# Seven products for part of the second expert chunk, with its sums of x made earlier, and a later spread of the first w2 maxima

## The chip, the cores and the metric

One core of a Trainium2 chip runs the whole program. The metric is the device time of one execution in microseconds (us); the median of three executions of the kernel before is 957.64 us (957.54 to 958.07).

## What is computed

The input is 2 x 8 heads of 768 tokens and 64 features. Attention inside clusters gives 1536 tokens of 512 features; a mixture of four experts and a second two-layer network follow. Cut to what matters here:

```python
x = attention(q, k, v, centroids)                  # 1536 x 512
p = domain_probs / domain_probs.sum(-1)            # 1536 x 4
for e in range(4):                                 # first network
    h = np.maximum(x @ w1[e], 0.0)                 # 1536 x 1024
    out += p[:, e:e + 1] * (h @ w2[e])
h = out @ w_in                                     # second network, 1536 x 2048
return np.maximum(0.01 * h, h) @ w_out
```

## The kernel before, in words

**Numbers.** Products of the two networks are made of 16-bit halves. A 32-bit matrix is scaled by a power of two, rounded to its high half on ScalarE (ACT), and the low half is the difference, made on GpSimd (POOL) or VectorE (DVE). Each product is then three matmuls on TensorE (PE): high x high, high x low, low x high. The scale comes from the largest entry: `peak` (L220, ACT) takes the maxima of each partition, `peak_across` (L224, PE) spreads them over the partitions with one small matmul, `peak_top` (L228 and `power`, DVE) takes the maximum of these and its power of two, and `weights_split` (L272, then `split_halves`, L264 and L267) scales and splits the weights.

**Chunks.** The hidden features are worked in chunks of 256: `N1` = 16 chunks of the experts (chunks 0 to 15) and 8 of the second network. A chunk has a first layer (x by w1, ReLU times p in `h_act`, L790 or L822, then halves of h in `split`, L139 and L140) and a second layer (`emit_y1`, L1195 to L1197: 12 blocks of 128 features by 512 tokens, each of six matmuls of 512 columns, copied or added into `acc` at L1203 and L1205).

**Two forms of the first layer.** In the plain form (`plain`, L1070) a chunk is 72 matmuls of 512 columns. In the form with seven products (`emit_seven`, `product`, L1059) w1 and x are seen as 2 x 2 blocks, x by halves of the features and by halves of the tokens (768 each), and seven products of blocks take the place of eight. It needs four sums of blocks of w1 (`weights_sums`, L284 to L287 on POOL, then their halves on ACT and POOL) and four of x (`input_sums`, L1013 on DVE, their high halves L1016 on ACT). The sums of x stay the same for all expert chunks. Before the change chunks 0 and 1 are plain and chunks 2 to 15 have seven products for all tokens. Two chunks of the second network have a mixed form (`full` is false): seven products for the 512 first tokens of each half (set A, 42 matmuls of 512 columns), plain ones for the other 256 of each half (set B, `plain_b`, L1119, 24 matmuls).

**Order.** Nothing is scheduled by a planner in this part: each engine works through its instructions in the order in which the program issues them, and waits on semaphores. Attention is written as a time line: `at(when, step)` entries, sorted by `when`; the pairs of constants in `PEAK_AT` place the maxima pass and the spread of chunk 0's w1 and w2 there. Chunk 0's first layer for tokens 0 to 1023 runs inside this time line (`h_products`, L775; `h_finish_early`, L822); its third block, tokens 1024 to 1535, is plain and comes after the attention pool `main` was closed (`st_main.close()`). Then the pool `ffn` is opened over the same memory; `raw64`, `sums`, `thi`, `tlo`, `part` and `acc_n` lie there. The temporaries `f` and `g` of `input_sums` are the two `raw64` tiles.

Between the blocks of a first layer and of a second layer the loop at the end of the kernel drops `steps`: small closures that carry the preparation of the next chunk and of the sums. `quota` says how many of the sums go into which stretch. In the second layer of a chunk whose successor has no spread inside `emit_seven` (`L1_POINT` false, as for chunk 0), the spread of the next w1's maxima follows the second block:

```python
emit_y1(c, i)
if i == (3 if c == N1 else 1) and more and not L1_POINT(c):
    peak_across(0, bank(1 if c == N1 - 1 else 6 if c == N1 or c >= FULL else 0))
    peak_top(c + 1, 0)
    weights_split(c + 1, 0)
```

Before the change the sums of x are 18 steps of 2 x 768 columns: 9 in the second layer of chunk 0, 6 in the first layer of chunk 1 and 3 in its second layer.

Of the kernel before, what the change touches and what calls it, by code (L numbers as in the profile page):

```python
# [8 lines left out]
F32 = mybir.dt.float32  # L9
# [4 lines left out]
AF = mybir.ActivationFunctionType  # L14
# [36 lines left out]
NORM_LAST = (6.49, 6.57)  # L51
PHI_LAST = ((0, 2, 4), (0, 2))
SPLIT_AT = (3.6, 7.0, 12.5)
PEAK_AT = ((4.6, 8.2), (18.1, 21.0))
FILL = ((0, 0, 1.07), (0, 6, 1.08), (0, 12, 6.38), (0, 18, 6.39), (1, 0, 9.94), (1, 6, 10.27), (1, 12, 10.27))

BIG = float(2 ** 60)
# [18 lines left out]
def attention_moe_kernel(  # L76
# [13 lines left out]
    nc = tc.nc  # L90
    B, H, S, D = q.shape
    C = centroids.shape[1]
    NT, DM = out.shape
    E, _, FE = w1.shape
# [12 lines left out]
    HT = NT // 2  # L107
# [67 lines left out]
    hbuf, gbuf, pbuf = [], [], []  # L175
# [3 lines left out]
    N1 = len(chunks)  # L179
# [3 lines left out]
    def weights_load(c, part):  # L183
        wa, wb, f0, e = chunks[c]
        r, n = (raw64, 2) if wide and e is None else (raw12, 1)
        if part == 0:
            src = wa[:, n * f0:n * (f0 + FCH)]
        else:
            src = wb[f0:f0 + FCH, :]
        nc.sync.dma_start(out=r[part], in_=src.rearrange("(k p) f -> p k f", p=128))  # L190
# [418 lines left out]
    def scaled_split(hi, lo, src, by):  # L609
# [12 lines left out]
        out=ident, in_=ident, pattern=[[1, 128]], compare_op=ALU.is_equal, fill=0.0,  # L622
# [6 lines left out]
    def warm(n):  # L629
# [10 lines left out]
        out=both.rearrange("p (t c) -> p t c", c=2 * C), in0=iv[:, :, 0, :], in1=iv[:, :, 1, :], op=ALU.add,  # L640
# [4 lines left out]
        out=par, in_=ident.rearrange("p (a h c) -> p h a c", h=2, c=C), op=ALU.add, axis=AX.XY,  # L645
# [12 lines left out]
        out=cw[:, 3:4], in0=cw[:, 0:1], scalar=cw[:, 2:3], in1=cw[:, 1:2], op0=ALU.mult, op1=ALU.add,  # L658
# [4 lines left out]
    for h in range(2):  # L663
        nc.vector.tensor_scalar(
            out=cpad[:, h, :], in0=craw, scalar1=cw[:, 5:6], scalar2=par[:, h:h + 1], op0=ALU.mult, op1=ALU.mult,
        )
    ps = small()
# [14 lines left out]
    for n in range(1, NQK):  # L682
# [11 lines left out]
        out=dp.rearrange("p (b j) e -> p b (j e)", b=B),  # L694
        in_=probs.rearrange("(b p j) e -> p b (j e)", b=B, j=J),
# [13 lines left out]
    steps = prep_argmax(0, 0)  # L709
# [3 lines left out]
    steps = prep_argmax(0, 1)  # L713
# [74 lines left out]
    def h_act(c, g, src, p):  # L788
        if c < N1:
            nc.vector.scalar_tensor_tensor(out=g, in0=src, scalar=0.0, in1=p, op0=ALU.max, op1=ALU.mult)  # L790
        else:
            nc.scalar.activation(out=g, in_=src, func=AF.Prelu, scale=H_DOWN, alpha=0.01)
# [9 lines left out]
    def like(x, y):  # L802
        return x if len(y.shape) == 2 else x.rearrange("p (u t) -> p u t", u=2)
# [75 lines left out]
    for pr in range(NPAIR):  # L879
        o = 2 * J * pr  # L880
        at(o + 3 * J + (X_AT if pr != NPAIR - 2 else X_LAST), emit_X, pr)
        if pr > 0:
            m = V_MOST_AT[pr]
# [78 lines left out]
    acc_n = ffn.tile([128, NTILE, DM], F32, name="accn")  # L962
# [3 lines left out]
    def is_wide(c):  # L966
        return wide and chunks[c][3] is None

    raw64 = [
        ffn.tile([128, KC, 2 * FCH], I32, name="w1raw64"), ffn.tile([128, FCH // 128, 2 * DM], I32, name="w2raw64"),  # L970
    ]
# [4 lines left out]
    part = ffn.tile([128, 2, NT // 2], F32, name="part")  # L976
# [22 lines left out]
    quarters = [[x[:, 2 * k:2 * k + 2, HT * u:HT * u + HT] for x in (xhi, xlo)] for k in range(2) for u in range(2)]  # L999

    t_hi, t_lo = [[t[:, 0], t[:, 1], quarters[1][n], t[:, 2]] for n, t in enumerate((thi, tlo))]

    def input_sums():

        sub, add = ALU.subtract, ALU.add
        b11, b12, b21, b22 = quarters
        f, g = [
            x.bitcast(F32).rearrange("p a b -> p (a b)")[:, 0:NT].rearrange("p (k t) -> p k t", k=2) for x in raw64
        ]
        e = part  # L1010

        def tt(out, in0, in1, op):
            return lambda: nc.vector.tensor_tensor(out=out, in0=in0, in1=in1, op=op)  # L1013

        def hi(n, src):
            return lambda: nc.scalar.activation(out=t_hi[n], in_=src, func=AF.Copy)  # L1016

        def lo(n, src):
            return tt(t_lo[n], src, t_hi[n], sub)

        return [
            tt(f, b12[0], b11[0], sub), tt(f, f, b12[1], add), tt(f, f, b11[1], sub),
            hi(0, f), tt(g, b22[0], f, sub), tt(g, g, b22[1], add), lo(0, f), hi(1, g), tt(e, b22[0], b12[0], sub),
            tt(e, e, b22[1], add),
            lo(1, g), tt(e, e, b12[1], sub), tt(f, b21[0], g, sub), tt(f, f, b21[1], add), hi(3, f),
            hi(2, e), lo(3, f), lo(2, e),
        ]

    def turn_sums(m):
# [44 lines left out]
    def emit_seven(c, steps, late):  # L1074
# [12 lines left out]
        u2, u3 = [{A: part[:, n, A], B: part[:, n, B]} for n in range(2)]  # L1087
        gB = [g_slot(2), g_slot(3)]

        full = c < N1 or c >= FULL  # L1090
        calls = [5 if full else 6]

        def some():
# [19 lines left out]
        def plain_b(f):  # L1113

            ps = bank(f)
            xs = [x.rearrange("p k (u t) -> p k u t", u=2) for x in (xhi, xlo)]
            for k in range(KC):
                for i, j in ((0, 0), (0, 1), (1, 0)):
                    nc.tensor.matmul(  # L1119
                        ps.rearrange("p (u t) -> p u t", u=2), lhsT=w[i][:, k, 128 * f:128 * f + 128],  # L1120
                        rhs=xs[j][:, k, :, 512:HT], start=k + i + j == 0, stop=k == KC - 1 and i == 1,
                    )
            h_act(c, gB[f], ps, None)
            hi, lo = [x[:, f, :].rearrange("p (u t) -> p u t", u=2)[:, :, 512:HT] for x in hbuf[0]]
            split(hi, lo, gB[f].rearrange("p (u t) -> p u t", u=2), nc.gpsimd)

# [151 lines left out]
    def mixed(*lists):  # L1278
        return [x for row in zip_longest(*lists) for x in row if x]

    PLAIN = (0, 1, N1, N1 + 1)
    FULL = N1 + 4
    sums_left, quota = [], []
    for c in range(NCH):
# [14 lines left out]
        if c in PLAIN:  # L1299
            if c != N1:  # L1300
                if c > 0:
                    weights_split(c, 1)
                out_scale(c)
            if c == N1:
                sums_left = turn_sums(slice(0, 512))
                quota = [0, 6, 4, 3]
            if c == 0:
                sums_left = input_sums()
                quota = [0, 9, 6, 3]
            n = quota.pop(0)  # L1310
            slots = mixed(sums_left[:n], steps)
            slots[len(slots) // 2:len(slots) // 2] = late[:1]
            if c != N1:
                slots += late[1:]
            sums_left = sums_left[n:]
            if c == N1:
                turn_max(1)
                for k in range(KC):
                    turn_split(1, k)
                weights_split(c, 1)  # L1320
            blocks = [(u, f) for u in range(2 if c == 0 else 0, NU) for f in range(NF)]
            for n, (u, f) in enumerate(blocks):
                if c > 0 and c != N1:
                    ps = bank(BANKS[u][f])
                    plain(c, u, f, ps)
                elif f == 0:
                    both_ps = [bank((BANKS[u] if c else LAST_BANKS)[f]) for f in range(NF)]
                    for k in range(KC):
                        for g in range(NF):
                            plain(c, u, g, both_ps[g], [k])  # L1330
                if c == N1 and n == 0:
                    turn_across(1, bank(1))
                    turn_scale(1)
                    for k in range(KC):
                        turn_split(2, k)
                    out_scale(c)
                if c == 0 or c == N1:
                    ps = both_ps[f]
                h_whole(c, f, ps, 512 * u, hl=[tokens(x[:, f], c, u, True) for x in hbuf[0]])
                if c == N1 and n < 2:  # L1340
                    continue
                for _ in range(-(-len(slots) // (len(blocks) - n))):
                    slots.pop(0)()
            left = []
        else:
            emit_seven(c, steps, late)
            left = steps

        steps, later = left, []
        if c == N1 + 2:  # L1350
            sums_left = turn_sums(slice(512, HT))
            quota = [5, 8]
        if c in PLAIN or N1 + 2 <= c < FULL:
            n = quota.pop(0)
            later, sums_left = sums_left[:n], sums_left[n:]
        if more:
            if not is_wide(c + 1):
                later.insert(0, lambda: peak(c + 1, 1))
            else:
                if c + 1 != N1:  # L1360
                    later.insert(0, lambda: peak(c + 1, 1))
                if c == N1:
                    later = late[1:] + later
                if c + 2 < NCH:
                    later.append(lambda: weights_load(c + 2, 1))
            if L1_POINT(c):
                steps.append(lambda: weights_split(c + 1, 0))
            else:
                steps.insert(0, None)
            if c + 1 not in PLAIN:  # L1370
                steps += weights_sums()
            if c + 2 < NCH and not is_wide(c + 2):
                steps.append(lambda: weights_load(c + 2, 0))
        if c == N1 - 3 and wide:
            steps += [lambda: weights_load(N1, 0), lambda: weights_load(N1, 1)]
        if c < N1 - 1 and c % (FE // FCH) == FE // FCH - 1:
# [66 lines left out]
```

## Time and profile before

| | us |
|---|---|
| median of three executions | 957.64 |
| the profiled execution | 957.70 |
| its span, first to last instruction | 955.8 |
| PE busy | 938.0 (98%) |
| DVE busy | 749.0 (78%) |
| ACT busy | 536.8 (56%) |
| POOL busy | 564.1 (59%) |

Times within the trace count from the start of the span. A row of a time line gives start, duration, engine, line, operation, what is written and read, the number of merged instructions, and in brackets how long the engine had stood idle and what released it. Matmuls overlap, so a row of PE may be longer than its share: a matmul of 512 columns lasts 0.38 us, and the next one starts 0.216 us after it did.

### The profile page before, as it was taken

Reading aid. Unit: us, or ns where it says so; the run is one execution under the profiler, and the core shown is the slowest. Engines: PE = TensorE matmul, PEld = TensorE weight load, DVE = VectorE, ACT = ScalarE, POOL = GpSimd, SP = SyncE. Lnnn points to the kernel's source line nnn. Section 1 sums busy time; section 2 is a strip of 40 time slices with the busy share of each in tenths; the row PEclk is TensorE's granted clock in tenths of the full one; section 3 lists DMA queues with packets and bytes.
Section 4 is the critical chain, followed back from the end, with each engine's and each line's share of the span. In section 5 each row is a group of like instructions: output and inputs, shape, how many; then the busy total and the mean of one; then the engine's idle time right before and its main releaser. Section 6 shows DMA issues by size and latency. Waiting matters only on the chain.

```text
span 955.8 us, 16375 instructions
## 1 busy us (share of the span) xinstructions
PE 938.0 (98%) x6423; PEld 552.2 (58%) x6456; DVE 749.0 (78%) x1286; ACT 536.8 (56%) x775; POOL 564.1 (59%) x456
## 2 busy tenths in 40 slices
PE   8899999999999999999999999999999999999998
PEld 5788888877545555555555555555544444455554
DVE  7989998889697676666766667666889978998865
ACT  3678777778555344334344343443579755566552
POOL 4467777780367565455654465654636667777672
PEclk9999999999999999999999999999999999999999
DMA  8785556550110112110211102114111211221103
GB/s 181 182 186 120 129 131 156 122 135 3 45 45 25 42 47 54 45 45 23 61 40 45 45 23 75 37 33 132 45 45 59 94 54 60 88 89 45 45 1 132
DMA packets 62245, 70.81 MB, mean 74 GB/s; under 512 B 28148, under 2 KB 44920, under 8 KB 62168
## 3 DMA queue, kind: packets, MB, share of 16 engines
q1 hardware_dynamic: 62168, 69.77, 27.0%
q8 instruction: 50, 0.82, 0.4%
q14 instruction: 27, 0.22, 0.1%
HBM read 46.19 MB, written 3.17 MB: 52 GB/s over the span
## 4 chain that ended last, share of the span: by engine, by line
PE 84%; DVE 11%; ACT 2%; DMA 1%; issue 1%; SPq 0%; DVEq 0%; ACTq 0%
PE z L1059 27%; PE z L1195 9%; PE z L1196 8%; PE z L1197 8%; PE z L1257 4%; PE z L1259 4%; PE z L1258 4%; PE z L1070 4%; PE big L508 3%; DVE m L512 2%; PE big L543 2%; PE big L544 2%; PE small L569 1%; PE small L570 1%; PE small L571 1%
## 5 line engine op out<-in xcount | busy, mean ns | idle before, releaser
L140 POOL TENSOR_TENSOR hlo<-g,hhi 128x512 bf16<-128x512 f32 x140 | 186.4, 1354 | 89.9 <-ACT hhi L139 89.9
L1205 DVE SCALAR_TENSOR_TENSOR acc<-z,outer,acc 128x512 f32<-128x512 f32 x180 | 133.8, 748 | 64.7 <-PE z L1197 64.7
L557 POOL TENSOR_TENSOR plo<-p,phi 128x768 f16<-128x768 f32 x83 | 136.2, 1652 | 68.3 <-ACT phi L556 38.6
L139 ACT ACTIVATE hhi<-g 128x512 f16<-128x512 f32 x140 | 86.6, 628 | 111.8 <-DVE g L790 110.2
L1195 PE MATMUL z<-hhi,w2hi 128*128 128x512 f16 x384 | 145.5, 379 | 1.6
L1196 PE MATMUL z<-hhi,w2lo 128*128 128x512 f16 x384 | 145.5, 379 | 0.0
L267 POOL TENSOR_TENSOR w2lo<-w2raw,w2hi 128x512 f16<-128x512 f32 x46 | 63.5, 1400 | 131.5 <-ACT w2hi L264 131.5
L1197 PE MATMUL z<-hlo,w2hi 128*128 128x512 bf16 x353 | 133.8, 379 | 0.0
L512 DVE TENSOR_REDUCE m<-big 128x1 f32<-128x768 f32 x96 | 89.9, 950 | 14.0 <-PE big L508 13.7
L546 ACT ACTIVATE p<-big 128x768 f32<-128x768 f32 x96 | 76.6, 808 | 34.6 <-PE big L544 28.6
L1059 PEld LDWEIGHTS <-shi 128*128 128x128 f16 x608 | 59.5, 98 | 41.3 <-issue 0.2
L1099 DVE TENSOR_TENSOR part<-z,part 128x512 f32<-128x512 f32 x76 | 41.2, 563 | 50.9 <-PE z L1059 48.3
L267 POOL TENSOR_TENSOR w1lo<-w1raw,w1hi 128x512 f16<-128x512 f32 x46 | 57.4, 1270 | 28.5 <-ACT w1hi L264 18.8
L1059 PE MATMUL z<-xx,shi 128*128 128x512 f16 (+1 forms) x304 | 73.1, 329 | 0.1
L1257 PE MATMUL z<-w2hi,hhi 128*128 128x512 f16 (+1 forms) x194 | 73.1, 377 | 0.1
L1059 PE MATMUL z<-xx,w1hi 128*128 128x512 f16 (+1 forms) x304 | 73.1, 329 | 0.0
L1259 PE MATMUL z<-w2hi,hlo 128*128 128x512 f16 (+1 forms) x194 | 73.1, 377 | 0.0
L1258 PE MATMUL z<-w2lo,hhi 128*128 128x512 f16 (+1 forms) x194 | 73.1, 377 | 0.0
L543 PE MATMUL big<-qka 128*128 128x512 f32 x192 | 70.0, 367 | 2.8 <-DVE m L512 1.2
L1266 DVE SCALAR_TENSOR_TENSOR accn<-z,outer,accn 128x512 f32<-128x512 f32 (+1 forms) x85 | 60.2, 736 | 14.5 <-PE z L1259 14.4
L264 ACT ACTIVATE shi<-sums 128x1024 f16<-128x1024 f32 x20 | 21.1, 1057 | 88.4 <-POOL sums L287 88.4
L790 DVE SCALAR_TENSOR_TENSOR g<-z,pb 128x512 f32<-128x512 f32 x92 | 51.7, 568 | 19.2 <-PE z L1059 11.4
(250 smaller groups left out, 2342.7 us busy)
## 6 DMA issues: line engine op xcount, KB each, us to landing
qkb<-pair SPq DMA_DIRECT2D x32, 384.0 KB
w1raw<-in_moe_w_dram SPq DMA_DIRECT2D x16, 512.0 KB
w2raw<-in_moe_w_dram SPq DMA_DIRECT2D x16, 512.0 KB
w1raw<-in_moe_w_in_dram SPq DMA_DIRECT2D x8, 1024.0 KB
w2raw<-in_moe_w_out_dram SPq DMA_DIRECT2D x8, 1024.0 KB
qka<-pair SPq DMA_DIRECT2D x16, 384.0 KB
qraw<-in_q_dram SPq DMA_DIRECT2D x16, 192.0 KB
kraw<-in_k_dram SPq DMA_DIRECT2D x16, 192.0 KB
```

Source lines behind the costliest of these rows:

```text
L140: lo_engine.tensor_tensor(out=lo, in0=src, in1=as_read(hi), op=ALU.subtract)
L267: nc.gpsimd.tensor_tensor(out=lo[:, x], in0=src[:, x], in1=hi[:, x], op=ALU.subtract)
L512: nc.vector.tensor_reduce(out=m_t[t][:, j:j + 1], in_=ps[:, 0:S], op=ALU.max, axis=AX.X)
L557: (nc.vector if plo_on_vector else nc.gpsimd).tensor_tensor(out=plo, in0=p, in1=phi, op=ALU.subtract)
L1059: nc.tensor.matmul(ps, lhsT=w[i][:, k, :], rhs=x[j][:, k, sub], start=first and k + i + j == 0, stop=k == 1 and i == 1, skip_group_check=True,
L1195: nc.tensor.matmul(out, lhsT=whi[:, f, ks], rhs=h, start=f == 0, stop=False)
L1196: nc.tensor.matmul(out, lhsT=wlo[:, f, ks], rhs=h, start=False, stop=False)
L1197: nc.tensor.matmul(out, lhsT=whi[:, f, ks], rhs=l, start=False, stop=f == NF - 1)
L1205: nc.vector.scalar_tensor_tensor(out=a, in0=out, scalar=by, in1=a, op0=ALU.mult, op1=ALU.add)
L1257: nc.tensor.matmul(ps, lhsT=hi[:, f, ts], rhs=whi[:, f, m], start=f == 0, stop=False)
L1258: nc.tensor.matmul(ps, lhsT=hi[:, f, ts], rhs=wlo[:, f, m], start=False, stop=False)
L1259: nc.tensor.matmul(ps, lhsT=lo[:, f, ts], rhs=whi[:, f, m], start=False, stop=f == NF - 1)
```

## The change

Chunk 1 gets the mixed form: seven products for set A (1024 tokens), plain ones for set B (512 tokens). The sums of x are made in two passes, first for set A (steps of 2 x 512 columns), then for set B (2 x 256 columns). The first five steps of set A are issued ahead of chunk 0's third block, the other 13 in chunk 0's second layer; set B has 8 steps in the first layer of chunk 1 and 10 in its second layer. Chunk 0's second layer also gets the sums of chunk 1's w1 and their halves, and chunk 2's w1 load goes behind them. The temporary `e` moves from `part` to `acc_n`, since `part` now holds products in chunk 1. The spread of chunk 0's w2 maxima goes from 21.0 to 23.9 in the time line of attention, from between two groups of the last head's output products to behind them.

```diff
-PEAK_AT = ((4.6, 8.2), (18.1, 21.0))
+PEAK_AT = ((4.6, 8.2), (18.1, 23.9))
...
-    def input_sums():
+    def input_sums(m):
 
         sub, add = ALU.subtract, ALU.add
-        b11, b12, b21, b22 = quarters
-        f, g = [
-            x.bitcast(F32).rearrange("p a b -> p (a b)")[:, 0:NT].rearrange("p (k t) -> p k t", k=2) for x in raw64
+        b11, b12, b21, b22 = [[x[:, :, m] for x in b] for b in quarters]
+        f, g, e = [
+            x.rearrange("p a b -> p (a b)")[:, 0:NT].rearrange("p (k t) -> p k t", k=2)[:, :, m]
+            for x in [*[r.bitcast(F32) for r in raw64], acc_n]
         ]
-        e = part
...
         return [
             tt(f, b12[0], b11[0], sub), tt(f, f, b12[1], add), tt(f, f, b11[1], sub),
-            hi(0, f), tt(g, b22[0], f, sub), tt(g, g, b22[1], add), lo(0, f), hi(1, g), tt(e, b22[0], b12[0], sub),
-            tt(e, e, b22[1], add),
-            lo(1, g), tt(e, e, b12[1], sub), tt(f, b21[0], g, sub), tt(f, f, b21[1], add), hi(3, f),
-            hi(2, e), lo(3, f), lo(2, e),
+            tt(g, b22[0], f, sub), hi(0, f), tt(g, g, b22[1], add), tt(e, b22[0], b12[0], sub), hi(1, g),
+            tt(e, e, b22[1], add), lo(1, g), tt(e, e, b12[1], sub), lo(0, f), hi(2, e),
+            tt(f, b21[0], g, sub), tt(f, f, b21[1], add), lo(2, e), hi(3, f), lo(3, f),
         ]
...
-        full = c < N1 or c >= FULL
+        full = 1 < c < N1 or c >= FULL
...
-            h_act(c, gB[f], ps, None)
+            if c < N1:
+                p = pbuf[0][:, 0, :].rearrange("p (u t) -> p u t", u=2)[:, :, 512:HT]
+                h_act(c, like(gB[f], p), like(ps, p), p)
+            else:
+                h_act(c, gB[f], ps, None)
...
-    PLAIN = (0, 1, N1, N1 + 1)
+    PLAIN = (0, N1, N1 + 1)
...
             if c == 0:
-                sums_left = input_sums()
-                quota = [0, 9, 6, 3]
+                sums_left = input_sums(slice(0, 512))
+                for _ in range(5):
+                    sums_left.pop(0)()
+                quota = [0, 16]
...
         else:
+            if c == 1:
+                sums_left = input_sums(slice(512, HT))
+                steps = steps[1:] + sums_left[:2] + steps[:1] + sums_left[2:8]
+                quota = [10]
+                sums_left = sums_left[8:]
             emit_seven(c, steps, late)
...
-        if c in PLAIN or N1 + 2 <= c < FULL:
+        if c < 2 or c in PLAIN or N1 + 2 <= c < FULL:
             n = quota.pop(0)
...
+            if c == 0:
+                steps = [None] * 4 + steps[1:5] + steps[6:] + [None] * 4 + steps[5:6]
```

## Rows read from the trace of the kernel before

**Rows 1.** The page, part 1: busy time of each engine.
```profile
PE 938.0 (98%) x6423; PEld 552.2 (58%) x6456; DVE 749.0 (78%) x1286; ACT 536.8 (56%) x775; POOL 564.1 (59%) x456
```

**Rows 2.** Windows: busy time and count per engine, granted clock, DMA share, GB/s.
```profile
250.00:260.00 10.00, 9.95 (x47) 4.56 (x47) 4.70 (x10) 5.75 (x11) 6.29 (x6) 1.00 0.00 0
```

**Rows 3.** The chain of work that ended last: start, duration, what.
```profile
271.02 15.54 PE z L1070 x72
...
775.41 1.29 PE z L1059 x6
...
788.37 1.29 PE z L1059 x6
```

**Rows 4.** Time line of PE around the spread of chunk 0's w2 maxima.
```profile
239.10 0.19 PE L571 MATMUL small<-vt,plo 128*128 128x65 f16 x1
239.89 0.22 PE L224 MATMUL small<-identb,pb 128*128 128x128 bf16 x1 [0.60 <-DVE xn L587]
...
241.60 0.59 PE L775 MATMUL big<-xx,w1hi 128*128 128x512 f16 x2
```

**Rows 5.** Time line of DVE, end of attention and chunk 0.
```profile
240.32 1.67 DVE L607 TENSOR_SCALAR xx<-xx,fold 128x1536 f16<-128x1536 f16 x3
...
245.13 1.23 DVE L140 TENSOR_TENSOR w2lo<-w2raw,w2hi 128x1024 f16<-128x1024 f32 x1 [1.42 <-ACT w2hi L139]
...
251.43 0.27 DVE L236 TENSOR_SCALAR outer<-pk,pk,most 128x1 f32<-128x1 f32 x1
254.75 1.40 DVE L790 SCALAR_TENSOR_TENSOR g<-z,pb 128x512 f32<-128x512 f32 x2 [3.06 <-PE z L1070]
258.05 0.29 DVE L228 TENSOR_REDUCE pk<-z 128x1 f32<-128x128 f32 x1 [1.90 <-PE z L224]
...
258.75 0.17 DVE L212 RECIPROCAL pk<-pk 128x1 f32<-128x1 f32 x1
258.83 1.74 DVE L1013 TENSOR_TENSOR w1raw<-xx 128x1536 f32<-128x1536 f16 x1
```

**Rows 6.** Time line of POOL, chunk 0's early blocks.
```profile
249.48 4.50 POOL L140 TENSOR_TENSOR hlo<-p,hhi 128x512 bf16<-128x512 f32 x4 [31.29 <-ACT hhi L139]
```

**Rows 7.** Time line of ACT in chunk 0.
```profile
256.96 0.19 ACT L220 ACTIVATION_READ_ACCUMULATOR junk<-w1raw 128x1 f32 x1
...
257.58 0.67 ACT L1203 ACTIVATE acc<-z,outer 128x512 f32<-128x512 f32 x1
...
259.75 1.14 ACT L272 ACTIVATE w1raw<-w1raw,pk 128x1024 f32<-128x1024 f32 x1
260.93 1.06 ACT L264 ACTIVATE w1hi<-w1raw 128x1024 f16<-128x1024 f32 x1
```

**Rows 8.** Time line of PE, chunk 0's second layer: its first matmul, and the spread.
```profile
255.20 0.38 PE L1195 MATMUL z<-hhi,w2hi 128*128 128x512 f16 x1
...
257.79 0.22 PE L224 MATMUL z<-identb,pb 128*128 128x128 bf16 x1
```

**Rows 9.** Time line of POOL, the sums of chunk 2's w1 and their low halves.
```profile
297.74 2.13 POOL L285 TENSOR_TENSOR sums<-sums,w1raw 128x256 f32<-128x256 f32 x1
299.83 0.73 POOL L286 TENSOR_TENSOR sums<-w1raw 128x256 f32<-128x256 f32 x1
...
302.41 2.27 POOL L267 TENSOR_TENSOR slo<-sums,shi 128x512 f16<-128x512 f32 x2 [1.17 <-ACT shi L264]
```

**Rows 10.** Time line of DVE at the same time.
```profile
297.20 2.08 DVE L1013 TENSOR_TENSOR xx<-part,xx 128x1536 f16<-128x1536 f32 x1
```

**Rows 11.** Time line of SP's queue: the load of w1 for chunk 3.
```profile
301.27 0.37 SPq L190 DMA_DIRECT2D w1raw<-in_moe_w_dram  x1
```

**Rows 12.** Time line of ACT: the maxima pass over that load.
```profile
306.61 1.04 ACT L220 ACTIVATE junk<-w1raw 128x1024 bf16<-128x1024 f32 x1
```

**Rows 13.** Time line of PE: the first matmuls of the kernel.
```profile
1.39 3.40 PE L633 MATMUL small<-zeros 128*128 128x512 bf16 x9 [1.39 <-POOL zeros L619]
```

More of the change, by code (lines that the diff above doesn't have):

```diff
@@ L1015, in hi @@
         def hi(n, src):
-            return lambda: nc.scalar.activation(out=t_hi[n], in_=src, func=AF.Copy)
+            return lambda: nc.scalar.activation(out=t_hi[n][:, :, m], in_=src, func=AF.Copy)
         def lo(n, src):
-            return tt(t_lo[n], src, t_hi[n], sub)
+            return tt(t_lo[n][:, :, m], src, t_hi[n][:, :, m], sub)
         return [
             tt(f, b12[0], b11[0], sub), tt(f, f, b12[1], add), tt(f, f, b11[1], sub),
-            hi(0, f), tt(g, b22[0], f, sub), tt(g, g, b22[1], add), lo(0, f), hi(1, g), tt(e, b22[0], b12[0], sub),
-            tt(e, e, b22[1], add),
-            lo(1, g), tt(e, e, b12[1], sub), tt(f, b21[0], g, sub), tt(f, f, b21[1], add), hi(3, f),
-            hi(2, e), lo(3, f), lo(2, e),
+            tt(g, b22[0], f, sub), hi(0, f), tt(g, g, b22[1], add), tt(e, b22[0], b12[0], sub), hi(1, g),
+            tt(e, e, b22[1], add), lo(1, g), tt(e, e, b12[1], sub), lo(0, f), hi(2, e),
+            tt(f, b21[0], g, sub), tt(f, f, b21[1], add), lo(2, e), hi(3, f), lo(3, f),
         ]
```

## The prediction

> **What bounds the kernel now.** I read the page first, then the windows, then PE's own waits. PE is busy for 98% of the span [rows 1], and in the stretch around the change it is busy for 9.95 us of 10 at a granted clock of 1.00, the 2.4 GHz level [rows 2]. From the first expert chunk on, PE waits for nobody, so each matmul taken away is time gained, and each time PE must wait is time lost that no later stretch gives back. The other engines matter only through what they hand to PE.
>
> The profiled execution took 957.70 us, 0.06 above the median of 957.64. The sum is made against 957.70 and then lowered by 0.06. About 0.2%, 1.9 us, is what a measurement can tell from no change: under 955.7 is faster, over 959.6 slower.
>
> **Part 1: products of chunk 1.** The plain first layer is 72 matmuls in 15.54 us. The form that chunk 1 gets (seven products for 1024 tokens, plain ones for 512) is 42 + 24 = 66 matmuls, and a chunk of the second network that has this form now runs from 775.41 to 789.66, 14.25 us [rows 3]. That is 1.29 us less. In that form there PE waits for nothing, so I cost the five additions of products on DVE at nothing; without that cover one of them (0.69 by the ReLU of the same shape in [rows 5]) would be the price.
>
> **Part 2: the later spread.** The spread of the w2 maxima is a matmul into the bank that head 14's output still holds, and PE stood idle 0.60 us for it: the matmul before began at 239.10, it at 239.89 [rows 4]. Put behind the last attention products it finds that bank free. The products of chunk 0 then start not at 241.60 but where the first of three rescalings of x, begun at 240.32 and 0.56 each, allows, near 240.99 [rows 4, 5]. Gain 0.61, between 0.5 and 0.8. DVE reads the spread's result only behind those rescalings, which end at 241.99 as before, so the scale of w2 is no later.
>
> **Part 3: five steps of the sums ahead of chunk 0's third block.** This is where time goes. DVE now gets four sums of 1024 elements (f three times, g once) in its queue before the two ReLUs of tokens 1024 to 1535, and ACT gets the high half of f before it turns to them. Queued behind that on ACT: the high half of the first ReLU, then the pass that takes the maxima of chunk 1's w1, then the rest. PE's spread of these maxima is the next matmul after the second block of the second layer and stops everything behind it.
>
> In the kernel before, DVE was free from 251.7 to 254.75 [rows 5], the ReLU started at 254.75, and 2.40 us later, at 257.15, the maxima were there [rows 5, 7]; PE wanted them at 257.79 [rows 8], so it had 0.6 to spare. Now everything is 0.61 earlier (part 2): PE wants them at 257.18. When do the sums begin? f lies in a pool laid over the closed attention pool, whose last readers are POOL's four subtractions 249.48 to 253.98 [rows 6]; a first writer of the new pool is ordered behind them. The trace of before shows no such wait, as its first writer came later. So I bound it: without the wait DVE starts at 251.1 (the end of the scale before it, 251.70 in [rows 5], less 0.61), with it at 253.45. I take the wait, since the program's order of pools demands it. One sum of 1024 elements takes 1.23 by the subtraction of that width [rows 5], 1.26 in a chain where each waits for the one before; three are done at 257.2, and behind the fourth the ReLU starts at 258.4. The maxima come 2.40 later, at 260.8, the spread at 260.9: **PE waits 3.7 us**. From below: with a start at 251.1 the ReLU starts at 256.0, the wait is 1.3. From above: 0.1 more for each sum and hand-over, 4.1.
>
> **Part 4: sums in chunk 0's second layer.** Behind the spread DVE has ten more sums, and POOL has the two low halves of w1 and now also the four sums of w1 and their low halves. Two rows say how they get on: POOL's sum of 128x256 took 2.13 in place of 0.73 [rows 9] while DVE's of 128x1536 was running, and that one took 2.08 [rows 10] in place of the 1.74 of a sum by itself [rows 5], having begun inside a POOL sum. One stands still while the other runs. Worked through in program order: the maxima's four small operations, 0.87 [rows 5], end at 262.0. ACT, with two copies of 0.67 and a maxima pass still before it, scales w1 (1.14) and rounds it (1.06) [rows 7] until 265.9, and makes the high half of g at 267.5. DVE did three sums meanwhile and waits for that. From then on they alternate: POOL's second low half to 268.2, then four times a DVE sum of 1.15 and a POOL sum of 0.7, until 275.5; the next small maxima until 275.6; the tenth step's sum until 276.8. ACT's last high half of x (1.06) stands before the last copy and before the high half of w1's sums, so that one is done at 279.5, and the first low half (1.14, half of the pair in [rows 9]) at 280.9. PE leaves the spread at 260.9, does ten blocks of 1.295 (255.20 to 257.79 is two, [rows 8]), waits 0.3 for a bank whose copy is late, enters chunk 1 at 274.3, does the first product (1.29) and the plain block (2.59), and at 278.15 wants the sums of w1: 1.4 for the high half, 0.9 after two matmuls for the low. **Together 2.6 us**; from below 0 (if they didn't stop each other, the low half would come at 278.1, in time), from above 3.6.
>
> **What moves without a price.** On SP's queue chunk 2's w1 load goes behind POOL's sums, to 275.5, and the w2 load behind it. Its reader, the maxima pass, ran 5.3 us after the issue in chunk 2 [rows 11, 12], so it is read by about 281, and the spread comes after five products and a plain block, at 284 or later. Without that cover it would cost up to one pass, 1.1. The 18 steps for tokens 512 to 767 of each half go into chunk 1 and its second layer; the elements are no more than before, and they are due only in chunk 2. Bound: one sum, 0.7.
>
> **Sum.** 957.70 - 1.29 - 0.61 + 3.7 + 2.6 = 962.1; against the median, 962.0. With the bounds of the two waits taken at half of their way this case runs from 960.4 to 962.8.
>
> **The rivals.** *Only the first wait.* POOL and DVE overlap better with these shorter operands, w1's sums come in time: 957.64 - 1.9 + 3.7 = 959.4, from 958.8 to 960.4. For it: the first low halves of w1's sums miss by 2.3 us only, in a chain of ten steps. Against it: [rows 9, 10]. Chance 0.15; half of it is slower by over 0.2%.
>
> *The sums start at once.* DVE begins at 251.1, POOL's subtractions don't stop it, nor do its sums later. The ReLU is at 256.0, PE waits 1.3 at the spread and nowhere else: 957.64 - 1.9 + 1.3 = 957.0. It decides where f's first writer starts, at 251.1 or behind POOL. For it: no row of before shows that wait; against it: the order of pools, and [rows 9, 10]. Chance 0.09.
>
> *The other side: the maxima are in time.* If the maxima pass of w1 got through ACT before the high half of f and the ReLU, PE would reach the spread with its maxima there, as now, and the two gains stand alone: 957.64 - 1.9 = 955.7, which I count as faster. It decides at 257.18: maxima by then, or not. For it: the 3.06 us of idle DVE that the sums fill [rows 5]. Against: four sums need 5.0, and ACT's queue is in that order. Chance 0.10.
>
> *The clock falls.* In the whole trace PE never stood idle as long as 3.7 us. The nearest rows are the kernel's first nine matmuls, after standing still: 3.40 us [rows 13], where nine of the usual pitch of 0.216 with a last one of 0.38 make 2.11: 1.3 us lost at the 1.2 GHz level. If PE came out of its wait like that: 962.0 + 1.3 = 963.3, from 962.3 to 963.8. Against it: the granted clock is 1.00 wherever PE had its short waits, but none of those is near 3.7. Chance 0.12. The Trainium skill (TensorE: Matmul & The Clock Gate, section "What's actually happening") says that the throttled clock is the default and that activity releases it, so that idling brings it back; no run here shows that yet. By that rule the time would be the 963.3 of this rival, without it 962.0.
>
> **How the numbers follow.** The main case has 0.54, the rivals 0.15, 0.09, 0.10 and 0.12. Slower by over 0.2%: 0.54 + 0.12 + half of 0.15, 0.74 rounded. Within: 0.09 and the other half, 0.16. Faster: 0.10. The predicted time is the main case's, 962.0. The range of 8 in 10 goes from the lower end of "only the first wait", 958.8, to the upper end of the falling clock, 963.8; it leaves out the two cases below, 0.19.
>
> **What would show it.** Right: the first layer of chunk 1 shows 66 matmuls in 14.25 us apart from waits; the 0.60 before the w2 spread is gone; PE's waits name the spread of w1's maxima in chunk 0 with 3 to 4 us, and the products of chunk 1 with 1 to 3 us, released by ACT and POOL; DVE's first sum starts as POOL's fourth subtraction ends; the ReLUs follow near 258.4. Wrong: a first sum at 251.1, or no wait of PE over 1 us between 255 and 285; then a gain of up to 1.9 stands. A granted clock under 1.00, or matmuls at half their pace behind the wait, would show the last rival.

## The result, and the profile after

The kernel after takes 962.61 us (median of five runs, 962.45 to 962.87) against 957.54 for the kernel before in the same comparison: ratio 1.0051, 95% interval 1.0039 to 1.0062. The change makes the kernel slower by 5.1 us; 962.0 was forecast. The profiled execution's span is 960.6 us, 4.8 more than before's 955.8.

The page of the kernel after, part 1 (beside [rows 1]):

```profile
PE 942.5 (98%) x6450; PEld 553.0 (58%) x6450; DVE 755.9 (79%) x1305; ACT 538.8 (56%) x781; POOL 564.5 (59%) x462
```

PE is busy 4.5 us longer with a program that has less for it to do. So the lost time is not to be found in its waits alone. Those are, by the view of waits (engine, line, what it waited for: us in total, times, longest), in the stretch that the change touches:

```profile
PE z L224 <- ACT junk L220: 3.4, 1, 3.4
PE z L1058 <- DVE g L1098: 0.2, 1, 0.2
```

The 0.60 us before the w2 spread [rows 4] is gone; 3.4 us before the spread of chunk 1's w1 maxima is new. The time line of PE shows what came behind it:

```profile
254.67 0.38 PE L1198 MATMUL z<-hhi,w2hi 128*128 128x512 f16 x1
...
257.05 0.38 PE L1200 MATMUL z<-hlo,w2hi 128*128 128x512 bf16 x1
260.85 0.29 PE L224 MATMUL z<-identb,pb 128*128 128x128 bf16 x1 [3.42 <-ACT junk L220]
260.93 0.63 PE L1198 MATMUL z<-hhi,w2hi 128*128 128x512 f16 x1
261.35 0.63 PE L1199 MATMUL z<-hhi,w2lo 128*128 128x512 f16 x1
...
266.44 0.38 PE L1199 MATMUL z<-hhi,w2lo 128*128 128x512 f16 x1
...
276.64 0.59 PE L1058 MATMUL z<-xx,w1hi 128*128 128x512 f16 x2
...
290.00 0.59 PE L1058 MATMUL z<-xx,shi 128*128 128x512 f16 x2 [0.18 <-DVE g L1098]
...
291.29 0.38 PE L1198 MATMUL z<-hhi,w2hi 128*128 128x512 f16 x1
```

The second layer of chunk 0 begins at 254.67, 0.53 earlier than before [rows 8], its two blocks of 1.295 end at 257.26, and the spread starts at 260.85. The 13 matmuls of 512 columns behind it, from 260.93 to 266.44, take 5.51 us; at the pitch of 0.216 they would take 2.81. The windows (columns as in [rows 2]; the number behind POOL's count is the granted clock) show it as a clock of 0.50, the 1.2 GHz level:

```profile
258.00:260.00 2.00, 0.00 (x0) 0.00 (x0) 1.69 (x3) 1.25 (x3) 0.17 (x1) 0.89 0.00 0
260.00:262.00 2.00, 1.16 (x4) 0.54 (x5) 0.73 (x5) 2.00 (x5) 1.54 (x2) 0.50 0.00 0
262.00:264.00 2.00, 2.00 (x6) 0.69 (x5) 2.00 (x3) 2.00 (x4) 0.60 (x1) 0.50 0.00 0
264.00:266.00 2.00, 2.00 (x6) 0.67 (x5) 1.97 (x2) 1.97 (x3) 0.30 (x1) 0.50 0.00 0
266.00:268.00 2.00, 2.00 (x10) 0.88 (x9) 0.90 (x2) 1.99 (x4) 2.00 (x2) 0.90 0.00 0
```

So four terms make the difference. The start of the second layer: -0.53. The wait: 260.85 - 257.26 = +3.6. The slow matmuls: 5.51 - 2.81 = +2.7. The first layer of chunk 1, from 276.64 to 291.29: 14.65 in place of 15.54 [rows 3], -0.89; of the forecast's 1.29 it loses 0.4 to a gap before 290.00, where a product's additions on DVE were late. Together +4.9. It stays to the end, as one row of each chain of waits tells (first a block of chunk 2 in the kernel after, then the same block before):

```profile
307.17 7.80 PE z L1058 x48
```

```profile
302.21 7.80 PE z L1059 x48
```

307.17 - 302.21 = 4.96. On DVE the kernel after shows the sums that stand ahead of the two ReLUs, as the prediction had them in its third part:

```profile
253.48 1.23 DVE L1013 TENSOR_TENSOR w1raw<-xx 128x1024 f32<-128x1024 f16 x1 [2.32 <-POOL hlo L140]
254.75 2.48 DVE L1013 TENSOR_TENSOR w1raw<-w1raw,xx 128x1024 f32<-128x1024 f32 x2
257.26 1.23 DVE L1013 TENSOR_TENSOR w2raw<-xx,w1raw 128x1024 f32<-128x1024 f16 x1
258.41 1.28 DVE L790 SCALAR_TENSOR_TENSOR g<-z,pb 128x512 f32<-128x512 f32 x2
```

The first waits for POOL's subtractions (line 140) until 253.48; the ReLUs follow at 258.41, not at 254.75 as in [rows 5].

### The profile page after: what moved, and what is told of

It is laid out like the page before. It is cut to its first block, busy times and chain, and to the rows that moved or that the text cites. A ratio compares the mean times of both kernels' runs of the same rounds, so it can differ in the third digit from the quotient of the medians.

```text
span 960.6 us, 16427 instructions
## 1 busy us (share of the span) xinstructions
PE 942.5 (98%) x6450; PEld 553.0 (58%) x6450; DVE 755.9 (79%) x1305; ACT 538.8 (56%) x781; POOL 564.5 (59%) x462
## 4 chain that ended last, share of the span: by engine, by line
PE 85%; DVE 11%; ACT 2%; issue 1%; POOL 1%; DMA 0%; ACTq 0%; DVEq 0%; POOLq 0%
PE z L1058 28%; PE z L1198 9%; PE z L1200 9%; PE z L1199 9%; PE z L1260 4%; PE z L1262 4%; PE z L1261 4%; PE big L508 3%; PE big L543 2%; DVE m L512 2%; PE big L544 2%; PE z L1069 2%; PE small L569 1%; PE z L1118 1%; PE small L571 1%; PE small L570 1%
## 5 line engine op out<-in xcount | busy, mean ns | idle before, releaser
L140 POOL TENSOR_TENSOR hlo<-g,hhi 128x512 bf16<-128x512 f32 x140 | 182.5, 1325 | 97.9 <-ACT hhi L139 94.4
L1200 PE MATMUL z<-hlo,w2hi 128*128 128x512 bf16 x384 | 146.6, 382 | 0.0
L267 POOL TENSOR_TENSOR w2lo<-w2raw,w2hi 128x512 f16<-128x512 f32 x46 | 61.2, 1351 | 126.7 <-ACT w2hi L264 126.6
L1058 PE MATMUL z<-xx,shi 128*128 128x512 f16 (+1 forms) x312 | 75.5, 330 | 0.2 <-DVE g L1098 0.2
L1058 PE MATMUL z<-xx,w1hi 128*128 128x512 f16 (+1 forms) x312 | 75.5, 330 | 0.0
L267 POOL TENSOR_TENSOR w1lo<-w1raw,w1hi 128x512 f16<-128x512 f32 x46 | 55.0, 1217 | 26.0 <-ACT w1hi L264 18.8
L1058 PEld LDWEIGHTS <-w1hi 128*128 128x128 f16 x468 | 45.2, 98 | 35.8
```

Source lines behind the costliest of these rows:

```text
L140: lo_engine.tensor_tensor(out=lo, in0=src, in1=as_read(hi), op=ALU.subtract)
L267: nc.gpsimd.tensor_tensor(out=lo[:, x], in0=src[:, x], in1=hi[:, x], op=ALU.subtract)
L1058: nc.tensor.matmul(ps, lhsT=w[i][:, k, :], rhs=x[j][:, k, sub], start=first and k + i + j == 0, stop=k == 1 and i == 1, skip_group_check=True,
L1200: nc.tensor.matmul(out, lhsT=whi[:, f, ks], rhs=l, start=False, stop=f == NF - 1)
```

## The experiments

The theory at the start: the sums of x for chunk 1 have no room on DVE, POOL and ACT in the time that they now have; the wait at the spread is only the first place where that shows. The rivals: the wait is all, and a better order would bring the gain; the fallen clock is all; the form of chunk 1 or the moved loads cost time themselves. All medians below stand beside a median of before from the same chip, between 957.6 and 957.9.

**The later spread alone** (the kernel before, one number):

```diff
-PEAK_AT = ((4.6, 8.2), (18.1, 21.0))
+PEAK_AT = ((4.6, 8.2), (18.1, 23.9))
```

> The kernel before with the later spread of chunk 0's w2 maxima alone (21.0 to 23.9). My reading: PE's idle time of 0.60 us before that spread is on the path, so it goes and the products of chunk 0 start 0.6 us earlier: 957.5 - 0.6 = 956.9, and no new wait of PE. Rival: the products wait for something else that ends just as late (the rescaling of x, the scale of w2), then 957.5.

956.94 against 957.73, ratio 0.9987 (0.9978 to 0.9996). The gain of this part is clear of the noise by itself, 0.8 where 0.6 was read, and the interval holds both.

**The steps ahead of the third block taken back, all or all but two** (the kernel after; the first of the two):

```diff
-                for _ in range(5):
-                    sums_left.pop(0)()
-                quota = [0, 16]
+                quota = [0, 18]
```

> The changed kernel with none of the five steps ahead of chunk 0's third block: all 18 steps of set A in chunk 0's second layer. My reading: PE's wait of 3.7 us at the spread of w1's maxima comes from the four sums in front of the two ReLUs on DVE, so it is gone here, PE never stands still long enough for its clock to fall, and the granted clock is 1.00 throughout. The sums are then later, and PE waits in the first layer of chunk 1 for sums of w1 and for the third sum of x, 2 to 3 us: 957.5 - 1.9 + 2.7 = 958.3. Rival: chunk 1's sums are in time by themselves (the changed kernel shows only 0.2 us of waiting there), then the two gains stand alone, 955.6. Second rival: the wait at the spread comes from something else (the load of w1, ACT), then it stays and the time is above 962.

> The changed kernel with two of the five steps ahead of chunk 0's third block instead of five. My reading: each sum there costs PE 1.25 us at the spread of w1's maxima beyond the 0.6 us that PE had to spare, counted from 253.5 where POOL's fourth subtraction ends; two make the ReLU start near 255.9 and PE wait 1.0 to 1.2 us. No fall of the clock. Together with 1 to 2 us of waiting in chunk 1 the time is 957.5 - 1.9 + 3.0 = 958.6. Rival: if the clock falls at any wait of that order, 2.7 more, 961.3. Rival: if chunk 1 waits for nothing, 956.7.

962.74 (1.0044, 1.0029 to 1.0058) and 963.04 (1.0049, 1.0034 to 1.0063): misses by 4.4 us, though each did at the spread what was expected. PE's waits from 250 to 300, first with no step ahead, then with two:

```profile
PE z L1058 <- ACT part L1132: 3.7, 1, 3.7
PE z L1058 <- DVE g L1098: 1.3, 1, 1.3
PE z L224 <- ACT junk L220: 1.1, 1, 1.1
```

```profile
PE z L1058 <- ACT part L1132: 2.2, 1, 2.2
PE z L1058 <- DVE g L1098: 1.5, 1, 1.5
PE z L224 <- ACT junk L220: 0.9, 1, 0.9
```

With no step ahead the whole loss has moved into chunk 1 (its line 224 is the spread for chunk 2). The time lines there, PE and ACT:

```profile
279.02 0.59 PE L1058 MATMUL z<-xx,w1hi 128*128 128x512 f16 x2 [3.71 <-ACT part L1132]
...
277.43 1.06 ACT L1016 ACTIVATE thi<-w1raw 128x1024 f16<-128x1024 f32 x1 [1.76 <-DVE w1raw L1013]
```

PE waits for a copy of line 1132, the copy stands on ACT behind the last high half of x, and that waits for a sum of DVE. The windows of the same kernel say why the sum is late:

```profile
260.00:270.00 10.00, 9.95 (x48) 4.57 (x48) 9.90 (x7) 7.01 (x10) 8.77 (x5) 1.00 0.01 2
270.00:280.00 10.00, 6.29 (x30) 2.71 (x29) 9.86 (x12) 6.31 (x8) 5.14 (x4) 1.00 0.20 52
280.00:290.00 10.00, 7.55 (x36) 3.20 (x34) 9.86 (x17) 3.88 (x7) 5.94 (x4) 1.00 0.17 53
```

DVE is busy for 9.9 of every 10 us (with the time in which a sum stands still beside POOL), and PE is busy for 6.29 and 7.55 of 10. Neither order brings the gain, and the wait at the spread doesn't look like a cost of its own.

**The clock held up.** The kernel after, with 16 matmuls of 512 columns in PE's stretch of waiting, whose results nobody reads:

```diff
+            if c == 0 and i == 1:
+                ps = bank(0)
+                for _ in range(16):
+                    nc.tensor.matmul(ps, lhsT=w2s[0][0][:, 0, 0:128], rhs=hbuf[0][0][:, 0, 0:512], start=True, stop=True)
```

> The changed kernel with 16 matmuls of 512 columns, whose result is overwritten, between the second block of chunk 0's second layer and the spread of w1's maxima: PE works through the 3.5 us that it otherwise stands still. My reading: the spread comes at the same moment as in the changed kernel, near 260.9, but the granted clock stays at 1.00, which gives back 2.7 us; the ten blocks behind it then end 2.7 us earlier, before the sums of chunk 1's w1 are there, and 1.8 to 2.6 us of that are lost again as PE waits in chunk 1 (ACT's high half, POOL's low half of the sums). Time 961.7 to 962.5. Rival: those sums are in time, then the whole 2.7 us are gained, 959.9. Second rival: the clock falls all the same, then 962.6.

962.62 (1.0043, 1.0028 to 1.0059), 0.1 above the range that was expected, with a granted clock of 1.00 in every window from 255 to 300. The 2.7 us of slow matmuls are gone, and nothing is won, since these waits have come:

```profile
PE z L1058 <- POOL slo L267: 0.9, 1, 0.9
PE z L1058 <- ACT shi L264: 0.8, 1, 0.8
PE z L1058 <- DVE g L1098: 0.7, 1, 0.7
```

2.4 us together, for the high and the low half of w1's sums and for a product's additions. The view counts a wait only from the end of the last matmul; by the rows that open chunk 1's two layers,

```profile
274.12 0.59 PE L1058 MATMUL z<-xx,w1hi 128*128 128x512 f16 x2
...
291.34 0.38 PE L1198 MATMUL z<-hhi,w2hi 128*128 128x512 f16 x1
```

the first layer takes 17.22 in place of 14.25, and 3.0 are lost. In the kernel after, PE enters chunk 1 2.5 us later, at 276.64, loses only 0.4 there, and leaves its first layer at the same moment, 291.29. The five runs of the kernel after say the same: their mean clocks are 0.996, 0.998, 1.000, 1.000 and 0.998, their times 962.61, 962.61, 962.45, 962.87 and 962.57. So the fallen clock isn't the cause of the loss in this kernel.

**The maxima in time, the sums still ahead** (the kernel after):

```diff
                 sums_left = input_sums(slice(0, 512))
+                steps.pop(0)()
```

> The changed kernel with one move: the pass that takes the maxima of chunk 1's w1 is issued ahead of the five sum steps, so that ACT does it near 252 and PE finds the maxima there. Reading after the first four runs: from 253.5 to the end of chunk 1's first layer DVE, with POOL, which can't run beside a DVE sum, is the bound; PE's wait at the spread is only where it first shows. So the 3.7 us and the fallen clock go, and waits of the same sum come later (at the blocks for tokens 1024 on, whose ReLUs are behind the sums, at the last block, at the sums of w1): 961.3 to 962.6. Rival: the wait at the spread was the loss, then the two gains stand, 955.7 to 957.5.

962.23 (1.0046, 1.0031 to 1.0061). No wait is left at the spread; in its place PE waits 2.0 for copies of the second layer's results (line 1206), 1.3 for the high half and 0.9 for the low half of w1's sums. That is as read, but the clock fell all the same in the profiled run, behind these shorter waits:

```profile
280.00:285.00 5.00, 5.00 (x16) 1.95 (x17) 3.89 (x5) 2.52 (x4) 5.00 (x4) 0.66 0.00 2
```

Here the fall seems to cost time: the two runs with a mean clock of 0.998 took 962.80 and 962.90, the two with 1.000 took 961.38 and 961.65. Even these are 3.6 us or more above before's 957.77.

**Own tiles for f and g**, so that the first sum need not wait for POOL (the kernel after):

```diff
+        xtmp.extend(early.tile([128, 2, NT // 2], F32, name=f"xtmp{n}") for n in range(2))
...
-            for x in [*[r.bitcast(F32) for r in raw64], acc_n]
+            for x in [*xtmp, acc_n]
```

> The changed kernel with f and g of the sums in tiles of their own, outside the memory of the closed attention pool, so that DVE's first sum needn't wait for POOL's fourth subtraction. Reading: it starts near 251.2 instead of 253.5, but the sums and POOL's subtractions then hold each other up in turn, so that four sums end only 0.2 to 0.4 us earlier, near 258.2; PE's wait at the spread is 3.1 to 3.5 us and the time 961.8 to 962.6. Rival: DVE and POOL run side by side, then four sums end at 256.1, PE waits 1.3 us at the spread, the clock does not fall, and the time is 960 or less.

962.18 (1.0045, 1.003 to 1.006). The first sum starts at 251.46, two us earlier, and the ReLUs still only at 258.05; the wait at the spread is 2.7, less than the 3.1 to 3.5 that were expected. The time lines of DVE and POOL show where the two us went:

```profile
252.71 4.15 DVE L1014 TENSOR_TENSOR xtmp<-xtmp,xx 128x1024 f32<-128x1024 f32 x2
...
249.32 6.46 POOL L140 TENSOR_TENSOR hlo<-p,hhi 128x512 bf16<-128x512 f32 x4 [30.68 <-ACT hhi L139]
```

Two sums take 4.15 in place of 2.48, POOL's four subtractions 6.46 in place of the 4.50 of [rows 6]. They take turns, one standing still while the other runs. The Trainium skill (SBUF — State Buffer, section "SBUF: two separate sides") calls the port pair that both use an exclusive lock, held for a whole instruction; these rows agree. The order of the pools, on which the prediction's third part rested, costs little beyond this: 0.7 us at the spread and 0.4 in the time.

**More sums**, in the kernel after (the first sum of e done four times) and in the kernel before (three times, 1536 elements wide):

```diff
+                sums_left[6:6] = [sums_left[6]] * 3
...
-                quota = [0, 16]
+                quota = [0, 19]
```

> The changed kernel with one sum of set A (the first of e, 128x1024, the same result each time) done four times instead of once in chunk 0's second layer: three more DVE operations of 1.2 us, longer where POOL works beside them. Reading: DVE with POOL is the bound there, so all of it comes out at the end: 962.6 + 3.6 to 4.7 = 966.2 to 967.3. Rival: the loss is the wait at the spread with the clock behind it, and DVE has room later: 962.6 to 963.5.

```diff
+                sums_left[8:8] = [sums_left[8]] * 2
-                quota = [0, 9, 6, 3]
+                quota = [0, 11, 6, 3]
```

> The kernel before with one sum (the first of e, 128x1536) done three times instead of once in chunk 0's second layer: two more DVE operations of 1.75 us, 3.5 us in the same stretch. Reading: there the sums are due only in chunk 2, so the stretch has room and PE still waits for nothing: 957.5 to 958.2. Rival: DVE is as much the bound in the kernel before, then about 961.

In the kernel after: 969.83 (1.0125, 1.011 to 1.0141), 7.2 us above it. Three sums of 1.23 are 3.7, up to 4.7 was expected; all of it comes out at the end, and more. What the rest is was not settled; the interleaving with the other steps changed too. In the kernel before: 959.69 (1.0021, 1.0011 to 1.003), about 1.9 of the 3.5 us that were added, where 0.5 at most was expected. Its time line of PE shows one of the new waits:

```profile
301.98 0.38 PE L1195 MATMUL z<-hhi,w2hi 128*128 128x512 f16 x1 [0.84 <-DVE acc L1205]
```

By these two figures the kernel before, with its sums due in chunk 2, had room for only some 1.6 us more, an estimate. The change cuts what is due at first to two thirds (sums of 1024 elements in place of 1536) and brings the due time forward by a whole chunk.

**The wait alone**, in the kernel before (the pass over w1's maxima done five times on ACT):

```diff
+            if c == 0:
+                steps = [lambda: [peak(1, 0) for _ in range(5)]] + steps[1:]
```

> The kernel before with the maxima pass of chunk 1's w1 done five times instead of once on ACT, so that PE waits at the spread of these maxima without any more work for DVE or POOL: four more passes of 1.04 us less 0.6 to spare, a wait of 3.6 us. This measures a wait of that length and the clock behind it by themselves. Reading: PE's clock falls to 0.5 as in the changed kernel, 2.7 us are lost in the matmuls behind, and as no other engine is the bound here, both come out: 957.6 + 3.6 + 2.7 = 963.9. Rival: the clock's fall costs nothing of its own, 961.2.

964.24 (1.006, 1.0043 to 1.0077). Time line and window:

```profile
262.29 0.23 PE L224 MATMUL z<-identb,pb 128*128 128x128 bf16 x1 [3.98 <-ACT junk L220]
...
264.00:266.00 2.00, 2.00 (x7) 0.65 (x5) 1.97 (x2) 1.98 (x4) 0.00 (x0) 0.50 0.00 0
```

A wait of 4.1 (258.15 to 262.29), and nine slow matmuls, from 263.00 to 266.63 in place of 9 x 0.216, another 1.7: together 5.8. The profiled run took 963.83, 5.9 above the 957.90 of before. The one run whose mean clock was 1.000 took 962.02, which is before's time and the wait of 4.1 alone. Where DVE has its sums due late, wait and clock do add up: nothing behind them swallows either.

**Fewer sums.** Two kernels leave the low halves of x out of the sums, six additions of ten for each half of the tokens (the expectation miscounts them as six of twelve); one keeps three steps ahead of the third block, the other none:

```diff
-            tt(f, b12[0], b11[0], sub), tt(f, f, b12[1], add), tt(f, f, b11[1], sub),
-            tt(g, b22[0], f, sub), hi(0, f), tt(g, g, b22[1], add), tt(e, b22[0], b12[0], sub), hi(1, g),
+            tt(f, b12[0], b11[0], sub),
+            tt(g, b22[0], f, sub), hi(0, f), tt(e, b22[0], b12[0], sub), hi(1, g),
...
```

> The kernel after, with six of the twelve elementwise sums and differences of x left out for each half of the tokens (every second addition on f, g and e; the first writes of f, g, e and f again, the high and low halves stay), so the sums of x hold only their first terms. Ahead of chunk 0's third block stand now two sums of DVE and one copy of ACT in place of four and one. Theory (the engine pair DVE and POOL has no room for the sums in the new place, and their amount alone makes the loss): DVE starts at 253.5 as before, the ReLU of the third block at 256.0, the spread has its maxima at 258.4, a wait of 1.2 us in place of 3.7; no fall of the granted clock; no later wait over 0.5. 957.6 - 1.9 + 1.2 = 956.9, between 956.3 and 957.8. Rival (the cost lies in the order of the steps, the moved loads or the form of chunk 1, not in the amount of the sums): the waits in chunk 1 stay, 960 or more.

> The same six sums left out for each half of the tokens, and no step of the sums ahead of the third block: the maxima of chunk 1's w1 are in time, and the sums come one step later each, but are half as many. Theory: no wait at the spread of these maxima; DVE has room; the waits that the same order showed with all sums (3.7, 1.3, 1.1) are gone or under 0.5 together; the two gains stand: 955.7, between 955.4 and 956.5. Rival (order, loads or form): 957.5 or more, with the wait for ACT in chunk 1 still there.

962.76 (1.0056) and 962.98 (1.0053): misses, but not for the rivals' reason. All waits of PE from 250 to 300, in the first kernel, then in the second:

```profile
PE z L1118 <- ACT xx L1016: 4.1, 1, 4.1
PE z L224 <- ACT junk L220: 0.9, 1, 0.9
```

```profile
PE z L1118 <- ACT xx L1016: 4.3, 1, 4.3
```

At the spread 0.9 of 3.7 us are left, or none, and none of the waits of chunk 1 named above. The 4.1 and 4.3 are of the experiment's own making: the shorter list for the second half of the tokens put its overwrite of a part of x ahead of the plain block that reads it. So the second half got its 18 steps back, and only the first half stayed short, with no step ahead:

```diff
+        return steps if m.start else [steps[i] for i in (0, 3, 4, 6, 7, 9, 11, 12, 13, 15, 16, 17)]
...
-                for _ in range(5):
-                    sums_left.pop(0)()
```

> The kernel after with six of the twelve elementwise sums left out for the first half of the tokens only, and no step of them ahead of the third block; the second half keeps all its 18 steps and their places. In the two runs with the short sums for both halves the places of the second half moved too: its last overwrite of x then stood ahead of the plain block that reads that part of x, and PE waited 4.1 and 4.3 us for it, with a clock fall behind; the waits of the first half were down to 0.9 and to none. Theory (the amount of the first half's sums makes the loss): no wait at the spread, none over 0.5 in chunk 1, clock 1.00, both gains stand: 955.7, between 955.4 and 956.8. Rival (order, loads or form cost time by themselves): 958 or more.

956.66 against 957.70, ratio 0.9989 (0.998 to 0.9998). One wait is left from 250 to 300, and the windows show PE at work where it stood before:

```profile
PE z L1059 <- DVE g L1099: 0.4, 1, 0.4
...
260.00:265.00 5.00, 5.00 (x25) 2.25 (x23) 1.85 (x2) 4.97 (x8) 3.44 (x4) 1.00 0.02 3
265.00:270.00 5.00, 5.00 (x25) 2.30 (x24) 4.83 (x7) 4.56 (x8) 3.81 (x3) 1.00 0.01 2
270.00:275.00 5.00, 5.00 (x25) 2.25 (x23) 3.83 (x6) 4.81 (x6) 2.19 (x2) 1.00 0.31 103
275.00:280.00 5.00, 5.00 (x25) 2.29 (x24) 4.97 (x7) 2.20 (x5) 4.97 (x4) 1.00 0.16 10
```

The form of chunk 1, the moved loads and the order are all still there. What is gone beside the kernel with no step ahead and all sums (962.74) is six DVE additions of about 1.23, 7.4 us, and with them 6.1 us of time. With the run of more sums, where the same place got more work and the loss grew, that shows the cause: it is the amount of the first half's sums against the time that they have. Six steps fewer also bring the steps between them forward a little; no run separates that.

How much the form gains by itself is another question. The later spread is in this kernel too, and it alone gave a ratio of 0.9987; 0.9989 can't be told from that. Only the trace shows a gain of the form, in the first layer of chunk 1:

```profile
270.28 0.60 PE L1059 MATMUL z<-xx,w1hi 128*128 128x512 f16 x2
...
285.14 0.38 PE L1199 MATMUL z<-hhi,w2hi 128*128 128x512 f16 x1
```

That is 14.86, less than before's 15.54, but 0.6 more than the 14.25 of 66 matmuls.

## Why the prediction was right

**Part 1, 1.29 fewer: 0.89.** The 66 matmuls took the 14.25 forecast apart from one gap of 0.4. "PE waits for nothing" in that form was the step that failed: the wait for DVE's additions of products (line 1098, or 1099 where a line was added) is there in six of the experiments with the new form too, with 0.4 to 1.5 us by the view of waits. The mixed chunk of the second network has no sums of x beside it on DVE; chunk 1 has.

**Part 2, 0.61: 0.53 here**, and 0.8 in the run of it alone. Right in the mean; a single profile says little, since the eleven profiled kernels with the later spread begin chunk 0's second layer anywhere from 254.30 to 255.36 (mean 254.73), the three without it from 255.20 to 255.56 (mean 255.35).

**Part 3, the wait of 3.7: 3.6.** Right at each station: first sum 253.48 (253.45 forecast), ReLU 258.41 (258.4), spread 260.85 (260.9). The choice between the two bounds for the first sum went by the order of the pools; the run with own tiles shows that the ReLUs would have come about as late without that order, since DVE and POOL take turns on these operands.

**Part 4, waits of 2.6: 0.2 named in the profile, and 2.7 of slow matmuls in their place.** With the clock held up, the waits are there, and nearly as large: of the 3.0 lost in chunk 1, 2.1 are for the two halves of w1's sums (2.3 forecast) and 0.8 for a product's additions, which part 1 had put at nothing; no wait for a bank (0.3 forecast) shows. In the kernel itself they did not come as predicted. The step that failed is in the rivals: the falling clock was priced at 1.3 and put on top, 963.3. It came, in the profiled run, at twice the price, and it added nothing, because it covers the same time: PE is slow while DVE, POOL and ACT catch up with the sums. So it is luck that the terms of the profile add up so well, as one 2.6 stood in for another; that the time itself is near 962 is not luck, since the sums set it with or without the fall.

**The deeper reading** was there only in pieces. The prediction treats the wait at the spread and the waits in chunk 1 as two terms. The runs show one: five arrangements of the same work (the kernel after, none or two steps ahead, the maxima first, own tiles), with PE's waits in quite different places, end between 962.2 and 963.0. The two runs of "the maxima first" in which the clock stayed up, 961.38 and 961.65, are the lowest single runs among them.

**Moved without a price** (loads, second half of the tokens): the last run has them all. Against the forecast gains of 1.9 it lacks 0.9; by its trace 0.6 is lost in chunk 1's first layer, nearly all of it at the wait for the additions, and chunk 2 begins at 300.86, 1.19 earlier than in the kernel before (302.05). So at nothing they were priced about right, as far as a run with fewer sums can tell.

The best version is the kernel before with the later spread alone, 956.94. The last run's 956.66 can't be told from it, and that kernel leaves part of the sums out.

## What to carry to other kernels

Products that are saved on TensorE are paid in sums on other engines, by a due time; count those engines' work between the earliest start and the due time, turns of DVE and POOL included, before counting the products. Where that work doesn't fit, reordering only moves the wait: try the same order with part of the work left out, and see whether the wait goes or moves. Losses that cover the same stretch (a slow clock, a late operand further on) must not be added: ask which of them would still be there without the other.

## What was not expected of the hardware

The price of a fallen clock after a standstill: 2.7 us in the kernel after, 1.7 in the run with late maxima, where the prediction had 1.3 from the kernel's first matmuls [rows 13]. The number of slow matmuls makes the price, 13 and 9 here. That those first matmuls ran at the 1.2 GHz level was read from their pitch alone; the windows over them show a granted clock of 1.00. In the kernel after the clock reads 0.50 from 260 until about 266.4.

The fall doesn't follow from one wait's length. PE waited 3.4 us in the kernel after and the clock fell; it waited 3.71 in the profiled run with no step ahead and it stayed at 1.00 in every window around, while the other five runs of that very kernel had mean clocks from 0.996 to 0.998. With two steps ahead and no wait over 2.2 us it fell: PE was busy for 2.80 us of the five before, and then, by the windows of that kernel,

```profile
280.00:285.00 5.00, 4.93 (x17) 1.78 (x16) 5.00 (x7) 3.43 (x5) 3.13 (x3) 0.66 0.00 2
```

The Trainium skill (TensorE: Matmul & The Clock Gate, section "What's actually happening") has idling bring the throttled clock back; most of these standstills agree, the 3.71 without a fall doesn't by its length alone. What decides in the single case stays open; no run was made for it.
